# A fixed instruction order with 59 exceptions, and a 512-wide last projection, in a fused attention and SwiGLU block

## The chip, the cores and the metric

The kernel runs on one core of a Trainium2 chip. The metric is the device time of one execution in microseconds (us). Ratios are given with a 95% interval. Engines are named as in the profile: PE (matmul), PEld (weight load), DVE (vector), ACT (activation), POOL and SP (which issues nearly all DMAs).

## The reference, cut to what matters

```python
S, D, H, Dh, F = 2048, 1024, 32, 32, 3584
sa, ca, ga, sb, cb, gb = six rows of silu(c) @ w_mod
h = layernorm(x) * (1 + ca) + sa
q = h @ wq              # 32 heads of 32
k, v = h @ wk, h @ wv   # one head, shared by all queries
p = softmax(q k^T / sqrt(32));  o = p v
x = x + ga * (o @ wo)
h = layernorm(x) * (1 + cb) + sb
x = x + gb * ((silu(h @ w1) * (h @ w3)) @ w2)
```

Everything is bf16. Two stages matter in what follows: the softmax, whose 2048 x 2048 x 32 exponentials all go through ACT, and the feed-forward part (FFN below), which is about half of PE's work.

## The kernel before: the parts that the argument touches

The kernel is a generator. It adds each instruction to a graph with its duration, its priority and what it reads and writes; then a list scheduler walks the graph with a model of time and **fixes the order of all engines before anything runs**. On the chip each engine works through its list, waiting on semaphores.

```python
def schedule(self, banks):
    ...
    while left:
        ...                      # the engine that can start something first
        if e == "pe":
            def key(c):
                s, n = c
                if n.cls == "S":             # score groups first
                    r = 0
                elif n.cls is not None:      # V: value matmuls, D: denominators
                    r = 1 if att or t - n.est > 1.0 else 4
                else:                        # F: projections, FFN
                    r = 3 if n.prio >= 4 else 0.5
                return (r, n.prio, n.seq)
        ...
        pick = min((c for c in cands if c[0] <= t + ...), key=key)
        ...
        if e == "pe" and self.warm is not None and t < self.warm[0]:
            ...                  # fills a hole with matmuls nobody reads
```

The 2048 queries are cut into 8 blocks of 256. A block has 64 *score groups*: eight matmuls into the banks set aside for scores (SP) in PSUM, the memory that matmuls write, read by two exps on ACT. While attention of one block runs, PE also has the output projection and the FFN of the block before it. All of this other work shares two PSUM banks (PB). Copying a result out of a bank is called its eviction.

```python
PB = [nc.alloc_psum_tensor("PB%d" % i, [P, 512], F32)[:] for i in range(2)]
...
def finish(f, h=None):            # for 4 heads (f) of a block
    g = grp()                     # takes one of the banks
    ...
        G.add("pe", vmm, ..., cls="V", mode="V", acq=g if w0 == 0 else None, groups=[(g, "w")])   # L983
    ...
        G.add("pe", dmm, ..., groups=[(g, "w")], mode="V", cls="D")                               # L1010
    ...
    G.add("dve", ... tensor_copy(ASB[:, f % 4, 0:qn], PB[g.bank][:, 0:qn]),
          groups=[(g, "r")], prio=1)                                                              # L1022
    ...
    G.add("dve", ... tensor_tensor(DSB[:, da, 0:qn], DSB[:, da, 0:qn], PB[g.bank][:, qn:2 * qn], ALU.add),
          groups=[(g, "r")], prio=1)                                                              # L1034
```

So the numerators and the denominators of four heads lie in one bank, and the bank is free only when DVE has copied the one (L1022) and added the other (L1034). Whoever comes next on PE and wants a bank waits for that.

The FFN of a block: the first two projections by tiles of 256 columns of `w1` and `w3`, each into a slot of a ring of six weight slots, then the second projection in four quarters of 256 columns, then two stores of 128 rows:

```python
for fp in range(NF // 2):
    sl, rk = ring()
    for w, src in enumerate((w1_in, w3_in)):
        dma(..., src[:, c0:c0 + 256] ..., ("ring", sl, w), nbytes=D * 512, clear=rk)
    for w in range(2):
        g = mm_group(2 * NC, gmm, ...)               # L1149, 16 matmuls of 256 columns
        ...                                          # DVE and ACT: tanh form of silu, product
for q in range(4):
    g = grp()
    for hf in range(2):
        dma(...)                                     # half of a quarter of w2
        ...                                          # L1183: 28 matmuls of 256 columns
    ...                                              # L1189, L1195: times gb, plus x
for t in range(t0, t0 + nt):
    dma(lambda e, t=t: e.dma_start(out2[t * P:(t + 1) * P, :], X[:, xs(t), :]), ...)   # L1201
```

The changed kernel has other line numbers. The same work stands at:

| work | before | after |
|---|---|---|
| score groups / exps | L923 / L933 | L960 / L970 |
| value matmuls / denominators | L983 / L1010 | L1026 / L1053 |
| DVE: numerators out / denominators added | L1022 / L1034 | L1065 / L1077 |
| query projection on PE / eviction by DVE | L663 / L666 | L700 / L703 |
| transposes on PE / eviction by DVE | L587 / L610 | L624 / L647 |
| first FFN projections | L1149 | L1199 |
| second projection, narrow / wide | L1183 / none | L1270 / L1241 |

The softmax here doesn't subtract the row's maximum and nothing guards it: scores larger than these inputs give would overflow.

## Time and profile before

| | before |
|---|---|
| median (lowest to highest) | 1147.71 us (1146.38 to 1148.85), 3 runs |
| span in the profile | 1144.24 us |
| start of score groups 1, 91, 129, 449 | 26.58, 199.81, 276.59, 907.15 us |
| start of the first FFN matmul, end of the last matmul | 199.49, 1139.82 us |
| from one block to the next (64 score groups) | 126.11 us |

The starts of score groups are a good ruler for this kernel: there are 512 of them, every kernel below has the same ones in the same order, and a difference between two kernels can be placed between two of them. "S91" below is the start of the 91st.

### The profile page before, as it was taken

How to read it: one execution, taken by the hardware profiler on the slowest of the kernel's cores; microseconds unless marked ns; L12 is line 12 of the kernel's file. 1: busy time of each engine (PE TensorE's matmuls, PEld its weight loads, DVE VectorE, ACT ScalarE, POOL GpSimd, SP SyncE). 2: the span in 40 equal slices, each digit the busy share in tenths (PEclk: the TensorE clock that was granted, in tenths of full speed). 3: DMA queues.
4: the chain of work that ended last, by engine and by line, in shares of the span. 5: the costliest groups of instructions: out<-in, count | busy, mean ns of one | idle time of the engine just before them, and what ended most of it. 6: DMA issues, size and time to landing. Idle time of an engine off the chain costs nothing.

```text
span 1144.2 us, 35491 instructions
## 1 busy us (share of the span) xinstructions
PE 1114.2 (97%) x15800; PEld 758.0 (66%) x15830; DVE 985.3 (86%) x1501; ACT 1024.9 (90%) x1167; POOL 43.6 (4%) x86
## 2 busy tenths in 40 slices
PE   7898998999999999999999999999999999999998
PEld 4564443767577666777567757776677757767887
DVE  6838899899989998999989998999989999997451
ACT  5999999999999999999999999999999999992110
POOL 3200001000100001000100000000100010000000
PEclk9999999999999999999999999999999999999999
DMA  9616102965596567865596558756785659656995
GB/s 331 191 58 203 39 1 66 286 190 168 121 294 190 163 172 193 232 172 164 151 254 199 163 144 237 206 165 183 163 250 169 183 121 282 196 154 187 293 292 152
DMA packets 385417, 211.09 MB, mean 184 GB/s; under 512 B 21745, under 2 KB 376049, under 8 KB 385265
## 3 DMA queue, kind: packets, MB, share of 16 engines
q1 hardware_dynamic: 383184, 208.69, 66.1%
q8 instruction: 124, 2.03, 0.8%
q10 hardware_dynamic: 2080, 0.13, 0.1%
q14 instruction: 29, 0.23, 0.1%
HBM read 201.46 MB, written 4.19 MB: 180 GB/s over the span
## 4 chain that ended last, share of the span: by engine, by line
PE 84%; ACT 9%; DVE 4%; POOL 1%; issue 1%; DMA 0%; SPq 0%
PE PB L1149 30%; PE PB L1183 16%; PE SP L923 12%; PE PB L983 10%; ACT UREG L933 8%; PE PB L1115 4%; PE SP L1149 3%; PE PB L663 3%; PE SP L1183 2%; PE PB L1010 2%; DVE UREG L956 1%; DVE QT L666 1%; DVE UREG L950 1%; DVE ST L530 0%; POOL RS L553 0%
## 5 line engine op out<-in xcount | busy, mean ns | idle before, releaser
L933 ACT ACTIVATE UREG<-SP 128x1024 bf16<-128x1024 f32 x1024 | 969.2, 1085 | 7.1 <-PE SP L923 5.2
L956 DVE TENSOR_TENSOR UREG<-UREG 128x2048 bf16<-128x2048 bf16 x240 | 292.4, 1218 | 11.1 <-ACT UREG L933 8.7
L1149 PE MATMUL PB<-QT,WREG 128*128 128x256 bf16 x1648 | 206.8, 273 | 2.0 <-DVE DSB L1034 2.0
L923 PE MATMUL SP<-QT,KT 32*128 32x256 bf16 x4096 | 203.5, 273 | 4.9 <-ACT UREG L933 4.7
L1149 PEld LDWEIGHTS PB<-QT,WREG 128*128 128x128 bf16 x1648 | 150.1, 98 | 46.6 <-issue 30.9
L950 DVE TENSOR_TENSOR UREG<-UREG 128x2048 bf16<-128x2048 bf16 x120 | 146.3, 1219 | 9.6 <-PE PB L1010 5.1
L923 PEld LDWEIGHTS SP<-QT,KT 32*128 32x128 bf16 x4096 | 60.8, 92 | 128.4 <-ACT UREG L933 75.4
L1149 PE MATMUL PB<-QT,HREG 128*128 128x256 bf16 x1056 | 134.1, 273 | 0.9 <-DVE DSB L1034 0.8
L983 PE MATMUL PB<-UREG,V 128*32 128x256 bf16 x4032 | 129.4, 274 | 3.4 <-DVE QT L610 1.2
L1149 PEld LDWEIGHTS PB<-QT,HREG 128*128 128x128 bf16 x1056 | 96.0, 98 | 30.1 <-issue 20.1
L983 PEld LDWEIGHTS PB<-UREG,V 128*32 128x32 bf16 x4032 | 98.1, 96 | 26.6 <-issue 17.7
L1183 PE MATMUL PB<-WREG,HREG 128*128 128x256 bf16 x812 | 100.6, 273 | 0.0
L1183 PEld LDWEIGHTS PB<-WREG,HREG 128*128 128x128 bf16 x812 | 75.5, 98 | 19.9 <-issue 11.0
L1149 PE MATMUL PB<-QT,X 128*128 128x256 bf16 x528 | 67.9, 274 | 0.0
L1183 PE MATMUL PB<-HREG 128*128 128x256 bf16 x532 | 67.3, 273 | 0.0
L663 PE MATMUL PB<-HREG,WREG 128*128 128x512 bf16 (+1 forms) x299 | 61.5, 338 | 3.7 <-DVE QT L666 1.6
L1158 ACT ACTIVATE GSB<-GSB 128x512 bf16<-128x512 bf16 x56 | 39.7, 709 | 27.5 <-DVE GSB L1156 27.5
L965 DVE TENSOR_TENSOR UREG<-UREG 128x2048 bf16<-128x2048 bf16 x52 | 63.4, 1219 | 0.6
L551 POOL TENSOR_SCALAR RS<-MV 128x1 f32<-128x1 f32 x32 | 20.6, 649 | 1004.2 <-DVE MV L532 1004.0
L1183 PEld LDWEIGHTS PB<-HREG 128*128 128x128 bf16 x532 | 49.3, 98 | 13.7 <-issue 7.8
L1158 ACT ACTIVATE WREG<-WREG 128x512 bf16<-128x512 bf16 x56 | 39.9, 713 | 20.0 <-DVE WREG L1156 20.0
L1149 PEld LDWEIGHTS PB<-QT,X 128*128 128x128 bf16 x528 | 48.2, 98 | 14.5 <-issue 9.5
(141 smaller groups left out, 1043.0 us busy)
## 6 DMA issues: line engine op xcount, KB each, us to landing
WREG<-in_B_w_dram SPq DMA_DIRECT2D x112, 512.0 KB, 5.3
HREG<-in_B_w_dram SPq DMA_DIRECT2D x74, 512.0 KB, 5.3
WREG<-in_B_w_dram SPq DMA_DIRECT2D x33, 896.0 KB, 5.1
X<-in_B_w_dram SPq DMA_DIRECT2D x38, 512.0 KB, 5.6
HREG<-in_B_w_dram SPq DMA_DIRECT2D x21, 896.0 KB, 5.1
X<-in_B_w_dram SPq DMA_DIRECT2D x10, 896.0 KB, 5.2
X<-in_A_x_dram SPq DMA_DIRECT2D x32, 256.0 KB, 5.3
WREG<-in_w_mod_dram SPq DMA_DIRECT2D x16, 512.0 KB, 4.6
```

Source lines behind the costliest of these rows:

```text
L663: g = mm_group(NC, lambda e, b, c: e.matmul(b[:, 0:n], WQ[:, c, f * P:(f + 1) * P], HT[:, c, sl], start=c == 0, stop=c == NC - 1), lambda ...
L923: r = e.matmul(SP[:, b, o:o + qn], KT[32 * gg:32 * gg + 32, kts[j] * P:(kts[j] + 1) * P], QT[32 * gg:32 * gg + 32, f, q0:q0 + qn], start=T ...
L933: G.add("act", lambda e, u=u, h0=h0, n=n, b0=b0, nb=nb: e.activation(U[:, u, h0 * W:(h0 + n) * W].rearrange("p (b w) -> p b w", b=nb), SP[ ...
L950: G.add("dve", lambda e, tr=tr, u=u, fu=first_u: e.tensor_tensor(TR[:, tr, 0:4 * W], U[:, fu, 0:4 * W], U[:, u, 0:4 * W], ALU.add), reads= ...
L956: G.add("dve", lambda e, tr=tr, u=u: e.tensor_tensor(TR[:, tr, 0:4 * W], TR[:, tr, 0:4 * W], U[:, u, 0:4 * W], ALU.add), reads=[("TR", tr) ...
L965: G.add("dve", lambda e, ta=ta, tb=tb: e.tensor_tensor(TR[:, ta, 0:4 * W], TR[:, ta, 0:4 * W], TR[:, tb, 0:4 * W], ALU.add), reads=[("TR", ...
L983: r = e.matmul(PB[g.bank][32 * gg:32 * gg + 32, 0:qn], V[:, kt, :], U[:, pu, (gg * npk + j) * qn:(gg * npk + j + 1) * qn], start=w0 + n == ...
L1010: r = e.matmul(PB[g.bank][32 * gg:32 * gg + 32, qn:2 * qn], SEL[:, ga, gj, :], a[:, (gg * npk + x % npk) * qn:(gg * npk + x % npk + 1) * q ...
L1115: g = mm_group(NC, lambda e, b, f, t=t, h=h: e.matmul(b, QT[:, f, t * P:(t + 1) * P], WO[:, f, h * 512:(h + 1) * 512], start=f == 0, stop= ...
L1149: return e.matmul(b[:, j * qn:(j + 1) * qn], w13[:, w, c, j * P:(j + 1) * P], QT[:, c, q0:q0 + qn], start=c == 0, stop=c == NC - 1)
L1158: G.add("act", lambda e, b=b: e.activation(TB[b], GS[b], ACT.Tanh, scale=0.5), reads=[("GS", b)], writes=[("TB", b)], clear=alias("TB") if ...
L1183: G.add("pe", lambda e, g=g, j=j, fc=fc, hf=hf, first=first, w2s=w2s: e.matmul(PB[g.bank][:, j * 256:(j + 1) * 256], HHT[:, hf * NH + fc, ...
```

## The change

Intent: let the order depart from the scheduler's rule in 59 places that a search had found, and make the last block's end shorter.

The scheduler numbers its choices. Where another kind of instruction could start at the same time, the entry of `CH` under that number says which alternative is taken; without an entry the rule holds. On DVE one alternative (`None`) is to hold the engine for 0.3 us.

```diff
+CH = {88: 2, 187: 1, 188: 1, 196: 1, 205: 1, 224: 1, 229: 1, 262: 1, 329: 2, 352: 1, 362: 1, 375: 1, 411: 1,
+      442: 1, 609: 2, 654: 2, 662: 1, 731: 1, 775: 1, 851: 2, 1272: 1, 1290: 2, 1463: 1, 1478: 1, 1492: 1, 1497: 1,
+      1526: 1, 1897: 1, 1915: 2, 2088: 1, ... , 3772: 1, 3790: 2,
+      3963: 1, 3978: 1, 3992: 1, 3997: 1, 4009: 1, 4163: 1, 4339: 1, 4342: 1, 4490: 1}
...
+    def choose(self, t, e, n, alts):
+        self.nch += 1
+        return CH.get(self.nch - 1, 0)
...
+            ch = self.choose(t, e, n, alts) if alts else 0
+            if ch:
+                if alts[ch - 1] is None:
+                    t_free[e] = t + 0.3
+                    continue
+                s, n = alts[ch - 1]
```

The second part loads weights for two tiles at a time (`w1` of both, then `w3` of both), and gives the buffers of the two tiles other places:

```diff
-        for fp in range(NF // 2):
-            sl, rk = ring()
+        for fd in range(NF // 4):
+            ws = []
+            for b in range(2):
+                sl, rk = ring()
+                ...
             for w, src in enumerate((w1_in, w3_in)):
-                dma(...)
+                for sl, rk, w13, c0 in ws:
+                    dma(...)
```

The third part is for the last block alone (`WIDE = (2,)`). Its second projection is 512 columns wide, in halves of four weight chunks, and each [128 x 512] of the output is stored as soon as it is done:

```diff
+        if wide:
+            NH = NF // 4
+            for h in range(2):
+                ...                                  # four chunks of w2, 512 columns each
+                for j in range(nt):
+                    g = grp()
+                    ...                              # 28 matmuls of 512 columns, L1241
+                    G.add("dve", ... O2B[:, ob], PB[g.bank], GBB[:, h * 512:(h + 1) * 512], ALU.mult ...)
+                    G.add("dve", ... X[:, sj, h * 512:(h + 1) * 512] ... ALU.add ...)
+                    dma(lambda e, ...: e.dma_start(out2[t * P:(t + 1) * P, h * 512:(h + 1) * 512], ...), ...)
```

Other additions of the diff (a second fold, a tanh over two tiles) are switched off.

## The prediction

> **What bounds the kernel now.** I read the page's totals and chain first, then the busy time by stretch, then the timeline at three places.
>
> ```profile
> PE 1114.2 (97%) x15800; PEld 758.0 (66%) x15830; DVE 985.3 (86%) x1501; ACT 1024.9 (90%) x1167; POOL 43.6 (4%) x86
> ...
> PE 84%; ACT 9%; DVE 4%; POOL 1%; issue 1%; DMA 0%; SPq 0%
> ```
>
> ACT at 90% is not a rival to PE over the whole span: it finishes its exps long before the end. The stretches (columns: PE, PEld, DVE, ACT, POOL busy with counts, clock, DMA share, GB/s) show where PE has holes:
>
> ```profile
> 122.00:163.00 41.00, 38.88 (x507) 17.69 (x512) 36.13 (x56) 40.39 (x44) 0.00 (x0) 1.00 0.01 2
> 180.00:200.00 20.00, 16.68 (x280) 8.19 (x280) 19.10 (x26) 19.35 (x22) 0.65 (x2) 1.00 0.34 90
> 200.00:1032.00 832.00, 827.70 (x11832) 567.22 (x11837) 772.59 (x1117) 828.92 (x942) 20.59 (x24) 1.00 0.70 192
> 1066.00:1140.00 74.00, 73.82 (x677) 65.90 (x674) 33.60 (x51) 8.81 (x14) 0.00 (x0) 1.00 0.98 249
> ```
>
> Before 200 us PE waits; after that it is full. The timeline of a middle block shows that the fullness is real:
>
> ```profile
> 600.37 2.03 PE L1149 MATMUL PB<-QT,HREG 128*128 128x256 bf16 x17
> 602.34 0.40 PE L923 MATMUL SP<-QT,KT 32*128 32x256 bf16 x8
> 602.66 1.27 PE L1149 MATMUL PB<-QT,HREG 128*128 128x256 bf16 x10
> ```
>
> From the starts: 17 matmuls and the change to the score group take 1.97 us, the score group and the change back 0.32. I went through the starts of all matmuls of this block: apart from one wait of about 0.2 us before an output projection and a gap of missing records, every step is 0.11 us, or 0.20 us where the tiling changes. **From the first FFN matmul (199.49 us) to the last (1139.8 us) the time is the sum of PE's work in its order.** ACT runs at 99.6% beside it, but no PE instruction waits for it beyond the cost of the change.
>
> Before 199.5 us the two alternate. Here (block 0's end):
>
> ```profile
> 151.66 0.40 PE L923 MATMUL SP<-QT,KT 32*128 32x256 bf16 x8
> 151.99 1.93 PE L983 MATMUL PB<-UREG,V 128*32 128x256 bf16 x64
> 153.85 0.40 PE L923 MATMUL SP<-QT,KT 32*128 32x256 bf16 x8
> 154.30 15.15 ACT L933 ACTIVATE UREG<-SP 128x1024 bf16<-128x1024 f32 x16 [0.25 <-PE SP L923]
> ...
> 196.05 0.40 PE L923 MATMUL SP<-QT,KT 32*128 32x256 bf16 x8 [0.47 <-ACT UREG L933]
> ```
>
> A lump of 64 value matmuls holds the next score group to 2.19 us, and ACT starves for 0.25; elsewhere PE waits 0.47 for ACT. One score group feeds two exps; the chain of waits has "230.20 7.33 ACT UREG L933 x8", so 0.917 us an exp and 1.834 us a group.
>
> **What the Trainium skill says.** "Perfetto Trace Analysis", Identifying the Most-Contended Engine: matmul busy share is not a good measure of nearness to the limit; therefore I used starts, not the 97%. "TensorE: Matmul & The Clock Gate", Back-to-back issue gap: N/2.4 + 2.5 ns when warm, so 109.2 ns for 256 columns and 215.8 for 512. The trace agrees: 56 matmuls in 6.11 us in the chain, and 24 of 512 columns in 5.18 us. "TensorEngine Tiling (Array Packing)", Key Properties: changing the tiling mode drains the engine. The trace agrees: about 0.09 us a change. "DMA: Bandwidth & Descriptors", Anatomy of one DMA: about 2.0 us fixed. The next-to-last output store took 2.04 us from issue to landing.
>
> **The change part by part.** I compared the built instruction orders, counting PE's groups. No arithmetic is taken out, except that the last block's second projection is 112 matmuls of 512 columns instead of 224 of 256.
>
> 1. *Picks before the first FFN matmul.* Both kernels do all query projections before it. I took each interval between score groups as the larger of 1.834 us and its PE content (0.216 us a 512-column matmul, 0.109 a 256, 0.027 a tile-packed one, 0.093 a change of tiling). Sums over intervals 1-20, 21-30, 31-50, 51-71, 72-80, 81-90: before 38.0, 19.7, 37.5, 40.5, 17.4, 18.5 = 171.6; after 37.9, 18.8, 37.4, 39.9, 16.9, 18.5 = 169.4. The trace has 173.2 (26.58 to 199.81 us), so the count misses 1.6 us of waits for other engines. The gain, 2.2 us, comes from lumps such as the 64 value matmuls, now cut in two around a score group (1.80 and 1.81 us of content, both hidden by the exps), and from query projections kept for the wait behind block 0's output projection, where the kernel before runs fillers (45 filler matmuls in all before, 38 after). But the first FFN matmul now follows the 91st score group instead of coming just ahead of it: 199.81 - 2.2 + 0.33 + 0.22 (one filler) = 198.2, so **-1.3 us** against 199.49.
> 2. *Waits that the count misses.* About 0.8 of the 1.6 us lies at intervals 81 and 82 (2.28 and 2.19 us for contents of 1.75 and 1.15), where value matmuls stand behind a transpose and wait for DVE's eviction. After, the transposes are split and the value work stands elsewhere. I take about half of the 1.6: **-0.7**.
> 3. *Picks from there on.* One score group fewer is left (-0.22); changes of tiling 924 before, 925 after (+0.09). The middle blocks have 141 changes each instead of 139, which the last block gives back. So the five picks that recur in every middle block are worth nothing on PE: **-0.1**. That 202 instead of 226 matmuls of block 6 remain after the last score group only moves ACT's end; PE does the same work.
> 4. *Wide second projection.* 224 x 0.1092 = 24.46 against 112 x 0.2158 = 24.17: **-0.3**. It reads four weight chunks in 6 us in its first pass, so they must be there early; six ring slots give it that.
> 5. *Stores per half.* The end now:
>
> ```profile
> 1139.86 0.69 DVE L1189 TENSOR_TENSOR WREG<-PB,GBB 128x512 bf16<-128x512 f32 x1 [4.96 <-PE PB L1183]
> 1140.58 0.42 DVE L1195 TENSOR_TENSOR X<-X,WREG 128x512 bf16<-128x512 bf16 x1
> 1141.04 0.83 SPq L1201 DMA_DIRECT2D out_dram<-X  x2
> ```
>
> The second store is issued 0.39 us behind the first and lands 2.7 us after 1141.04. After, one store of half the size remains: no second issue, and some 0.3 us less to move. **-0.8**.
>
> Sum: -3.2 us of 1147.7, so 1144.5.
>
> **Rivals.** *A new wait in the middle.* DVE is 93% busy there and the order on every engine is fixed; a moved addition that ends late would stop PE seven times. For: five picks recur per block, and cutting value lumps brings bank releases nearer to their users. Against: the kernel before shows hardly a wait in such a block. At 0.3 us a block: +2, so 1146.5. *The search hits more than I count*: PE's waits and fillers before 200 us are some 15 us by my sum; if a third goes, 1142. *The weight stream becomes the bound at the end*: it runs at about 290 GB/s from 1060 to 1120 us, DMA share above 1; loads are now issued in pairs of tiles, and the wide pass wants 3.7 MB at twice the pace. Against: no PE wait for a DMA there now, and 1 KB rows instead of 512 bytes. If it misses, +2 to +5 us. *ACT bounds the middle*, so a smoother exp stream counts: 126.1 us a block against 128 x 0.917 + 14 x 0.52 = 124.6 would give 1.5 us a block, 10 in all. Against: PE shows no wait to give back.
>
> **Range and chances.** The parts are each uncertain by about 1 us, the runs before spread over 2.5 us, and the rivals pull both ways: 1144.5 with 1141.5 to 1147.4. Two per cent is 23 us; the waits and the tail together hold less than that, so faster by 2% is nearly excluded, and slower by 2% needs a stall of 3 us in each block, which nothing suggests.
>
> **What would show it.** Step 1: the 91st score group near 197 us, first FFN matmul near 198. Step 3: a middle block still 126.1 to 126.3 us, PE without waits. Step 4: the last projection in 24.2 us without a gap. Step 5: from last matmul to the end 3.6 us instead of 4.4. The prediction is wrong if a block's period falls below 125.5 us (then ACT, not PE, bounded it) or rises above 126.8 (a new wait).

## More of the kernel before

The prediction reads the totals, the stretches and the timeline. Here is a view that it doesn't show: what PE waited for. The columns are what waited and its line, what it waited for, the sum in us, how many times, and the longest.

```profile
PE SP L923 <- ACT UREG L933: 4.7, 12, 0.7
PE PB L1149 <- DVE DSB L1034: 2.8, 7, 0.4
PE PB L663 <- DVE QT L666: 1.6, 3, 0.8
PE PB L983 <- DVE QT L610: 1.2, 1, 1.2
PE PB L1115 <- issue: 1.1, 7, 0.2
PE PB L983 <- DVE QT L666: 1.1, 1, 1.1
```

Read it by the count in the middle. Twelve waits of 4.7 us in total are PE waiting for exps. The third, fourth and sixth line are PE waiting for DVE to empty a bank, a few times in the whole execution. The second line and the fifth come seven times, and so does the FFN beside an attention block: eight blocks, and all but the last have their FFN beside the next one's attention.

## The result, and the profile after

The changed kernel takes **1139.26 us** (median of 6 runs, 1138.17 to 1139.95), the kernel before 1147.21 in the same rounds (6 runs, 1146.38 to 1148.85). The ratio is 0.9929, 95% 0.9916 to 0.9942. The gain of 7.9 us is real, under two per cent, and more than twice the 3.2 us predicted; 1139.26 lies below the range.

Totals and chain of the changed kernel's page, beside those in the prediction:

```profile
PE 1117.9 (98%) x15711; PEld 745.9 (66%) x15711; DVE 986.4 (87%) x1501; ACT 1021.6 (90%) x1167; POOL 41.4 (4%) x86
...
PE 84%; ACT 12%; DMA 2%; DVE 1%; POOL 1%; issue 0%; SPq 0%; DVEq 0%
```

DVE's share of the chain fell from 4% to 1%, and DMA's rose from 0% to 2%. Both point to something below. The stretches (PE, PEld, DVE, ACT, POOL busy with counts, clock, DMA share, GB/s):

```profile
180.00:200.00 20.00, 16.91 (x281) 8.76 (x281) 19.97 (x27) 20.00 (x23) 0.00 (x0) 1.00 0.44 114
200.00:1032.00 832.00, 831.80 (x11850) 569.71 (x11851) 775.88 (x1121) 824.92 (x938) 19.58 (x24) 1.00 0.70 193
```

In the second row PE is busy for 831.80 of 832.00 us. The row of the kernel before, in the prediction, has 827.70. I had read that as full; it had a hole of 4.3 us by the profile's own count.

**What the hole was.** The timeline of a middle block of the kernel before (start, duration, engine, line, operation, output and input, count, and in brackets the idle time before and who ended it):

```profile
642.58 0.39 PE L1010 MATMUL PB<-UREG,SEL 128*32 128x256 bf16 x8
...
642.91 0.40 PE L923 MATMUL SP<-QT,KT 32*128 32x256 bf16 x8
643.03 0.42 DVE L1022 COPY XN<-PB 128x256 f32<-128x256 f32 x1 [0.50 <-PE PB L1010]
...
643.24 0.28 PE L1149 MATMUL PB<-QT,X 128*128 128x256 bf16 x1
643.37 0.41 DVE L1034 TENSOR_TENSOR DSB<-DSB,PB 128x256 f32<-128x256 f32 x1
...
643.92 0.82 PE L1149 MATMUL PB<-QT,WREG 128*128 128x256 bf16 x6 [0.41 <-DVE DSB L1034]
```

From the last matmul of one FFN group (643.24) to the first of the next (643.92) it is 0.69 us in the unrounded starts, where 0.11 is the usual step: 0.58 us lost. (The bracket says 0.41, since it counts from the modelled end of the matmul.) The new group needs a bank; one is held by the group that has just ended, the other by the values and denominators, and it is free when the addition at L1034 ends, at 643.78. When I wrote the prediction I took this step for missing records. The waits view names it, seven times: 2.8 us by its way of counting, and 7 x 0.58 = 4.1 us by starts. So the hole of 4.3 us isn't made of this alone: 2.8 us of it are these waits, and most of the rest are gaps of 0.16 us before output projections, where a record is missing and no time was lost (below). That 4.1 and 4.3 lie close together is chance.

The same place in the changed kernel:

```profile
640.12 0.40 PE L960 MATMUL SP<-QT,KT 32*128 32x256 bf16 x8
...
640.45 0.62 PE L1026 MATMUL PB<-UREG,V 128*32 128x256 bf16 x16
...
640.89 0.39 PE L1053 MATMUL PB<-UREG,SEL 128*32 128x256 bf16 x8
...
641.22 0.83 PE L1199 MATMUL PB<-QT,WREG 128*128 128x256 bf16 x6
...
641.98 0.40 PE L960 MATMUL SP<-QT,KT 32*128 32x256 bf16 x8
```

Behind the denominators there are now six matmuls of an FFN group that already has its bank, then a score group; the bank is asked for later, when DVE is done. No bracket is left. The block's period fell from 126.11 to 125.77 us: 0.58 given back, less two more changes of tiling in a block (141 instead of 139, some 0.09 us each), which leaves 0.40 where 0.34 was measured.

What PE waits for in the changed kernel, the lines that answer to those above:

```profile
PE SP L960 <- ACT UREG L970: 5.7, 15, 1.1
...
PE PB L1199 <- DMA WREG<-in_B_w_dram: 1.2, 1, 1.2
...
PE PB L700 <- DVE QT L703: 0.5, 1, 0.5
```

The addition of denominators is gone from the list, waits for the query projection's eviction are down from 1.6 and 1.1 us to 0.5, and there is a new line: one wait for a weight load. It stands at the first FFN tile:

```profile
198.44 0.40 PE L960 MATMUL SP<-QT,KT 32*128 32x256 bf16 x8 [0.46 <-ACT UREG L970]
200.08 2.91 PE L1199 MATMUL PB<-QT,WREG 128*128 128x256 bf16 x13 [1.24 <-DMA WREG<-in_B_w_dram]
202.92 0.61 PE L960 MATMUL SP<-QT,KT 32*128 32x256 bf16 x8
```

PE now reaches `w3` of the first tile before the load has landed. A second thing is to be seen here: 13 matmuls took 2.91 us, where 13 x 0.109 and the change of tiling are about 1.5. PE ran at half its clock for 3.41 us from 200.2 us on. That is not part of the change; other profiles here have it at other places or not at all, and it cost this one about 1.8 us (below).

The end of the changed kernel:

```profile
1134.73 0.69 DVE L1247 TENSOR_TENSOR WREG<-SP,GBB 128x512 bf16<-128x512 f32 x1 [4.61 <-PE SP L1241]
1135.52 0.42 DVE L1251 TENSOR_TENSOR X<-X,WREG 128x512 bf16<-128x512 bf16 x1
1135.97 0.33 SPq L1254 DMA_DIRECT2D out_dram<-X  x1
```

The DVE work is as long as before, but one store of half the size is left and landed 1.70 us after issue. From the last matmul (1134.69) to the end of the span (1138.16) it is 3.47 us, before it was 4.42.

### The profile page after: what moved, and what is told of

Read it like the earlier page. It is cut to its first block, busy times and chain, and to the rows that moved or that the text cites. A ratio compares the mean times of both kernels' runs of the same rounds, so it can differ in the third digit from the quotient of the medians.

```text
span 1138.2 us, 35291 instructions
## 1 busy us (share of the span) xinstructions
PE 1117.9 (98%) x15711; PEld 745.9 (66%) x15711; DVE 986.4 (87%) x1501; ACT 1021.6 (90%) x1167; POOL 41.4 (4%) x86
## 4 chain that ended last, share of the span: by engine, by line
PE 84%; ACT 12%; DMA 2%; DVE 1%; POOL 1%; issue 0%; SPq 0%; DVEq 0%
PE PB L1199 29%; PE PB L1270 14%; PE SP L960 13%; ACT UREG L970 12%; PE PB L1026 9%; PE PB L1158 5%; PE PB L700 3%; PE SP L1199 3%; PE SP L1270 2%; PE PB L1053 2%; PE SP L1241 1%; PE PB L1241 1%; DMA WREG<-in_B_w_dram 1%; ACT WREG L1207 1%; PE SP L1158 1%; DMA WREG<-in_w_mod_dram 1%
## 5 line engine op out<-in xcount | busy, mean ns | idle before, releaser
L1026 PE MATMUL PB<-UREG,V 128*32 128x256 bf16 x4096 | 132.9, 274 | 1.2 <-ACT UREG L970 1.0
L1207 ACT ACTIVATE WREG<-GSB 128x512 bf16<-128x512 bf16 x112 | 74.9, 669 | 45.1 <-DVE GSB L1204 45.1
L1270 PE MATMUL PB<-WREG,HREG 128*128 128x256 bf16 x700 | 88.6, 273 | 0.0
L1270 PEld LDWEIGHTS PB<-WREG,HREG 128*128 128x128 bf16 x700 | 64.0, 98 | 19.2 <-issue 11.8
L1219 DVE SCALAR_TENSOR_TENSOR HREG<-WREG,HREG 128x512 bf16<-128x512 bf16 x112 | 75.8, 677 | 0.9
L1204 DVE CAST GSB<-PB 128x512 bf16<-128x512 f32 x104 | 70.7, 680 | 4.4 <-PE PB L1199 3.5
L1214 DVE TENSOR_TENSOR HREG<-GSB,PB 128x512 bf16<-128x512 bf16 x98 | 66.3, 676 | 6.0 <-PE PB L1199 5.6
L700 PE MATMUL PB<-HREG,WREG 128*128 128x512 bf16 (+1 forms) x312 | 65.1, 340 | 0.9 <-DVE QT L703 0.5
L1270 PE MATMUL PB<-HREG 128*128 128x256 bf16 x476 | 61.2, 273 | 0.0
```

Source lines behind the costliest of these rows:

```text
L700: g = mm_group(NC, lambda e, b, c: e.matmul(b[:, 0:n], WQ[:, c, f * P:(f + 1) * P], HT[:, c, sl], start=c == 0, stop=c == NC - 1), lambda ...
L1026: r = e.matmul(PB[g.bank][32 * gg:32 * gg + 32, 0:qn], V[:, kt, :], U[:, pu, (gg * npk + j) * qn:(gg * npk + j + 1) * qn], start=w0 + n == ...
L1204: G.add("dve", lambda e, g=g, b=b: e.tensor_copy(GS[b][:, 0:2 * qn], PB[g.bank][:, 0:2 * qn]), writes=[("GS", b)], groups=[(g, "r")], dur= ...
L1207: G.add("act", lambda e, b=b: e.activation(TB[b], GS[b], ACT.Tanh, scale=0.5), reads=[("GS", b)], writes=[("TB", b)], clear=alias("TB"), d ...
L1219: G.add("dve", lambda e, fp=fp, b=b: e.scalar_tensor_tensor(HHT[:, 2 * fp:2 * fp + 2, 0:qn], TB[b][:, 0:2 * qn].rearrange("p (j q) -> p j ...
L1270: G.add("pe", lambda e, g=g, j=j, fc=fc, hf=hf, first=first, w2s=w2s: e.matmul(PB[g.bank][:, j * 256:(j + 1) * 256], HHT[:, hf * NH + fc, ...
```

## The experiments

Theories, by the letters that the expectations use. **A**: the picks ahead of the first FFN matmul are most of the gain; the picks that recur in every block give 0.35 us each, and the last projection and its stores 1.2. **B**, the rival: the picks of the middle blocks are most of it, 4 us or more. **C**: the layout does it (weight loading in pairs, buffers, the wide projection), not the order. The prediction itself had held a fourth view, that the middle picks are worth nothing. The later calls have theories of their own, on the load and on the start. Four kernels on one chip, five rounds each, with the kernel before at 1147.72 us (9 runs).

### No picks at all

```diff
-CH = {88: 2, 187: 1, ... , 4490: 1}
+CH = {}
```

> The changed kernel with the 59 picks taken out: wide last projection, half stores, paired weight loads and the new sigmoid buffers alone. Theory A (the picks in the first 200 us remove PE's waits and ACT's hunger, and that is most of the gain): 1146.0 us, that is 1.2 under the kernel before (0.3 for the wide matmuls, 0.9 for the last store), the 91st score group at 199.8 us and a middle block at 126.1. Theory B (the picks of the middle blocks do it): the same 1146.0. Theory C (the layout does it, not the order): 1141 or less.

Measured: 1146.26 us (1145.62 to 1146.73), ratio 0.9984 (0.9972 to 0.9997). The blocks' period is 126.11 us as before, the wait for the denominators is there seven times, and the last stretch, from S449 to the last matmul, takes 232.39 us instead of 232.67. So the wide projection gives 0.28 us, the half stores shorten the tail from 4.42 to 3.48, and C falls: without picks 1.2 us by the trace (1.5 by the medians) is all there is. A and B both had 1146.0, so this run doesn't separate them. The profile had a stretch at half clock at 105.5 us.

### Only the picks up to number 851

```diff
-CH = {88: 2, ... , 851: 2, 1272: 1, ... , 4490: 1}
+CH = {88: 2, ... , 851: 2}
```

> Only the 21 picks that fall before the first FFN matmul. Theory A: the 91st score group at 194.8 us as in the changed kernel, the first FFN matmul at 195.3, about 4 us below the kernel without picks, so 1142.0; less what the late weight load at 198 us takes back. Middle blocks at 126.1. Theory B: at most 1 to 2 us below the kernel without picks, so 1144.5.

Measured: 1142.11 us (1140.97 to 1145.54), ratio 0.995 (0.9936 to 0.9963). Of the waits of PE:

```profile
PE PB L1199 <- DVE DSB L1077: 2.4, 6, 0.4
...
PE PB L1199 <- DMA WREG<-in_B_w_dram: 0.9, 1, 0.9
```

The list has 20 entries, not the 21 of the expectation. The wait for the load is there, and without picks it wasn't, so the early picks bring it about. The wait for the denominators is there six times of seven, and the period is 126.11. By the medians the gain is 5.6 us, where the changed kernel has 7.9; what is missing must come from later picks. The profiled execution, 1145.54, is the slowest of the five: it had three units of 3.41 us at half clock, from 37.9 and 102.7 us.

### All but the last nine picks

```diff
-CH = {88: 2, ... , 3790: 2, 3963: 1, 3978: 1, 3992: 1, 3997: 1, 4009: 1, 4163: 1, 4339: 1, 4342: 1, 4490: 1}
+CH = {88: 2, ... , 3790: 2}
```

> All picks but the last nine, those of the last block. Theory A: the middle blocks go to 125.77 us, 0.35 less each in five blocks, so about 1.5 below the kernel with the early picks: 1140.5. The rest to 1139.3 is the last block. Theory B: the step from the early picks to this one is 4 us or more.

Measured: 1140.69 us (1139.11 to 1141.02), ratio 0.9932 (0.9919 to 0.9944). The period is 125.76, and of the two waits in question this is left:

```profile
PE PB L1199 <- DMA WREG<-in_B_w_dram: 1.0, 1, 1.0
...
PE PB L1199 <- DVE DSB L1077: 0.4, 1, 0.4
```

The one that is left stands at 1016 us, in the last block, whose picks were taken away. B is refuted, since the step from the early picks is 1.4 us by the medians and not 4, and so is the prediction's own view: blocks whose picks are kept lose the wait and 0.35 us of their period, and the block whose picks are gone keeps the wait. From S449 to the last matmul it is 232.04 us, against 231.13 in the changed kernel: the last nine picks are worth 0.91 us, of which 0.58 is the wait, and three changes of tiling fewer (928 to 925 from the first FFN matmul on) are about 0.3.

### The last projection narrow again

```diff
-    WIDE = (2,)
+    WIDE = ()
```

> The changed kernel with all picks, but the last block's second projection 256 wide and its rows stored whole. The orders of all engines are the same up to that projection. Theories A and B: 0.3 for the matmuls and 0.9 for the store are lost, 1140.5 us. Theory C: 3 us or more are lost.

Measured: 1139.79 us (1139.42 to 1141.27), ratio 0.9933 (0.992 to 0.9945). In the trace the last stretch is 0.29 us longer (231.42 instead of 231.13) and the tail is 4.42 us again instead of 3.48; from S449 to the end of the span it is 235.84 us, in the changed kernel 234.62. The medians show 0.5 against the changed kernel. It was run at another time. Medians don't resolve this here, the trace does. C, which had 3 us or more, falls here too.

On another chip: what the wait for the load costs, and whether it can be had back. The kernel before took 1146.54 us there (9 runs). All of these five-round runs keep the changed kernel's order on PE, ACT and DVE.

### The changed kernel again

> The changed kernel once more, unchanged, beside the next three on the same chip: 1139.3 us. If its profile holds no stretch at half clock, the 129th score group is at 272.5 us instead of 274.3, and the span about 1136.5.

Measured: 1139.03 us (1138.48 to 1140.07), ratio 0.9931 (0.9917 to 0.9944), as in the first measurement. PE waits 0.9 us for the load, and this time runs at full clock there. Its stretch at half clock is elsewhere:

```profile
98.00:101.80 3.80, 3.15 (x69) 1.77 (x68) 3.46 (x5) 3.10 (x5) 0.00 (x0) 1.00 0.56 182
101.80:105.20 3.40, 3.40 (x18) 0.90 (x16) 2.56 (x5) 2.75 (x4) 0.00 (x0) 0.51 0.96 329
```

The column behind POOL is the granted clock: 1.00, then 0.51 for 3.4 us, with PE busy through all of it. Interval S31 to S51 is 38.85 us here and 37.00 to 37.12 in profiles of the same order without such a stretch, so it costs 1.7 to 1.9 us. With one in the profile, the expected span of 1136.5 wasn't put to the test.

### `w3` of the first tile ahead of `w1` of the second

```diff
+    u, v = firstw[1], firstw[2]    # the 2nd and 3rd weight load of the first FFN
+    sp[u.pos], sp[v.pos] = v, u    # exchanged in the DMA queue, after scheduling
```

> The changed kernel with two weight loads of the first FFN exchanged in the DMA queue (the first tile's second weight ahead of the second tile's first), every engine's order frozen. Theory A (what the early picks won is partly given back by a late weight load at 198 us): PE's wait of 1.2 to 1.3 us for that load goes, the way from the 91st to the 129th score group falls from 77.8 to about 76.9, and the time is 1 us lower, 1138.3. Rival (that wait lies beside ACT's pace and costs nothing): no change.

Measured: 1138.41 us (1137.85 to 1139.38), ratio 0.9927 (0.9915 to 0.994). The same place as above:

```profile
199.72 0.40 PE L960 MATMUL SP<-QT,KT 32*128 32x256 bf16 x8 [0.46 <-ACT UREG L970]
200.05 1.59 PE L1199 MATMUL PB<-QT,WREG 128*128 128x256 bf16 x13
```

No bracket stands on the second line any more, and 13 matmuls take 1.59 us. S91 to S129 is 76.95 us, against 77.6 to 77.8 in the profiles with the wait and without half clock there, and 76.78 in the kernel before. So the wait costs 0.7 to 0.9 us, most of the 0.8 to 1.1 that the waits view shows for it in those profiles, and the rival falls. It takes two things together: PE that comes earlier (without picks there is no such wait) and the pairing, by which `w3` of the first tile stands third in the queue.

### The first tile's weights in a slot that is free early

```diff
+    RING[0], RING[5] = RING[5], RING[0]    # the first tile takes the slot that is free from about 50 us
...
+    for n, (was, now) in firstw[:12]:      # after scheduling: wait for the old contents of the new slot
+        n.deps = [d for d in n.deps if id(d) not in was] + list(now.values())
+    # and the first loads sorted anew in the DMA queue, both of the first tile in the two early places
```

> The changed kernel with the first tile's weights in the ring slot that is free from about 50 us (the sixth tile's stood there), every engine's order frozen. Theory A: the first FFN matmuls never wait for a load, 1 to 1.3 us lower than the changed kernel, 1138.0; with fewer stretches at half clock perhaps 1137.5. Rival: the sixth tile's load now comes in the crowded queue and makes PE wait near 215 us instead: no gain or a loss.

Measured: **1137.85 us** (1137.73 to 1139.91), ratio 0.9925 (0.9913 to 0.9938). No wait for a load is left, S91 to S129 is 76.96 us. Four of the five runs lie at 1137.7 to 1137.9; the fifth has a mean clock of 0.998 and 1139.91. This is the best version of the study, and beats both kernels: its median is 1.2 us below the changed kernel's of the same call. The intervals of the two ratios overlap, so it is the trace, with 0.7 to 0.9 us less between S91 and S129, that says where it comes from. Part of the rest is half clock: among the runs with a mean clock of 1.000 the two kernels are 1.06 us apart (1137.82, four runs, and 1138.88, three). The load of the sixth tile made PE wait nowhere, so the rival falls.

### Only the picks up to 442

```diff
-CH = {88: 2, ... , 442: 1, 609: 2, ... , 4490: 1}
+CH = {88: 2, ... , 442: 1}
```

> Only the 14 picks up to number 442, which reach to about the 50th score group. Theory A: the way to the 51st group is as in the changed kernel, 1.8 us shorter than before; of the rest of the 5.0 us at the 91st group (1.5 between groups 51 and 72, 0.4 to 81, 1.3 to 91) most is missing, so the 91st group is near 198 us where no half clock falls. Rival (the first picks set up all that follows): the 91st group at 195.

One look: 1142.65 us. S91 stands at 196.65, with a stretch at half clock before it, so about 195 without: the rival was right. I had expected that a part of S91's gain would need the picks from 609 on; it doesn't, and the builds show that picks numbered over 442 change nothing on PE ahead of the 92nd group. So the question of what sets up the gain at the start is one about the first 14 picks.

Three shorter lists, with one run of the kernel before at 1145.96 us. They were run at other times.

### Only the first pick; the first 8; the first 12

```diff
-CH = {88: 2, ... , 4490: 1}
+CH = {88: 2}                               # p88
+CH = {88: 2, 187: 1, ... , 262: 1}         # p262
+CH = {88: 2, 187: 1, ... , 375: 1}         # p375
```

> The first pick alone (it moves vector statistics and some value projections among score groups 3 to 15). Counting PE's content by interval, as in the prediction, it is worth 0.1 us; if it also takes away waits, as I now think, the 21st score group comes 0.6 us earlier, at 38.05 us after the first, and the 91st at 172.6 after the first (173.2 before). A stretch at half clock adds 1.4 to 2 us where it falls, and is told from the clock records.

> The first eight picks. By the count of contents 1.4 us of the 2.2 at the 91st score group. If the picks' real worth is the waits, the way from the first to the 31st group is 56.7 us (58.4 before), but from the 81st to the 91st it is still about 19 us, since value matmuls stand behind the transposes there: the 91st at 170.5 to 171.5 after the first.

> The first twelve picks. The twelfth puts query projections and split transposes between groups 81 and 88, so the way from the 81st to the 91st falls from 19.3 to 18.0 us; the 91st group 168.4 us after the first, as good as all picks (168.2). Rival (the last two early picks hold a share): 169.5.

Measured: 1146.56, 1145.47 and 1141.26 us, single runs. The intervals between score groups tell more (us; a star marks a stretch at half clock inside, which adds 1.4 to 1.9):

| groups | before | first 1 | first 8 | first 12 | first 14 | all |
|---|---|---|---|---|---|---|
| 1 to 21 | 38.63 | 40.55* | 40.06* | 38.71 | 40.00* | 38.05 |
| 21 to 31 | 19.79 | 19.79 | 18.62 | 18.55 | 18.54 | 18.63 |
| 31 to 51 | 37.18 | 37.30 | 37.43 | 37.02 | 37.02 | 37.12 |
| 51 to 72 | 41.00 | 41.00 | 40.36 | 39.50 | 39.47 | 39.48 |
| 72 to 81 | 17.34 | 17.34 | 18.43 | 16.92 | 16.90 | 16.90 |
| 81 to 91 | 19.29 | 19.28 | 18.66 | 18.13 | 18.03 | 18.03 |
| sum | 173.23 | 175.26* | 173.56* | 168.83 | 169.96* | 168.21 |

The first pick alone moves nothing that can be seen (the interval that it could change is hidden by the half clock). The first eight shorten 21 to 31 by 1.2 and 51 to 72 by 0.6, and lose 1.1 at 72 to 81; a new wait of 2.0 us of a score group for an eviction (L647) stands at 189 us, within 81 to 91. Without the half clock S91 would come some 171.6 to 172.2 us after S1, later than the 170.5 to 171.5 expected. With four more, 173.23 becomes 168.83: nearly all of the early gain, as expected. The last two add at most 0.6, and the first interval alone scatters by 0.4 between profiles with all picks (38.05 to 38.47). So the early gain isn't one event: the first eight picks give about a quarter of it, and with those from 329 to 375 nearly all is there. Whether the latter would give their part without the first eight wasn't tested.

## Why the prediction was wrong

The sum of terms, without half clock, in us. "Measured" is from the traces of before and after and of the experiments.

| term, by the prediction's steps | predicted | measured |
|---|---|---|
| steps 1 and 2, at the first FFN matmul | -2.0 | -4.2 |
| the same, at S91 | | -5.0 |
| late first weight load, S91 to S129 | 0 | +0.9 to +1.0 |
| step 3, S193 to S449 (four blocks) and the last stretch without its own nine picks | -0.1 | -1.4 and -0.35 |
| step 3, the last block's picks | in the above | -0.9 |
| step 4, wide projection | -0.3 | -0.3 |
| step 5, tail | -0.8 | -0.9 |
| sum (from S91: -5.0 + 0.95 - 1.4 - 0.35 - 0.9 - 0.3 - 0.9) | -3.2 | -7.9 |

The -5.0 is the difference of two profiles; four others with all early picks and no half clock there (to 3790, narrow, and the two with moved loads) have S91 at 168.3 to 168.6 us after S1, so 4.6 to 4.9.

**What bounds the kernel: right but for 4.1 us, by one wrong sentence.** PE's work in its order does set the time from the first FFN matmul on, all but seven waits; ACT at 99.6% did not keep the period from falling. The sentence that failed is "apart from one wait of about 0.2 us before an output projection and a gap of missing records, every step is 0.11 us, or 0.20 us where the tiling changes". I had the two exchanged. The "gap of missing records" was the wait of 0.58 us for the denominators, seven times over. The "wait of about 0.2 us" before the output projection was the missing record: one matmul of 512 columns takes 0.216 us, and the count there is one short. The waits view had both, on its second and fifth line; the second is said to be ended by DVE, the fifth by "issue", that is by nothing.

**Steps 1 and 2 together had 2.9 us at S91, and it was 5.0.** By stretches as in step 1, the count of content had 0.1, 0.9, 0.1, 0.6, 0.5 and 0 us; the traces fell by 0.6, 1.2, 0.1, 1.5, 0.4 and 1.3. Step 1's method has a flaw: taking the larger of ACT's 1.834 us and PE's content in each interval *by itself* overcounts, since where PE has little to do it runs ahead of ACT (in the kernel before, S88 comes 1.63 us after S87), and what it has put in front of ACT covers a longer interval after it. So 171.6 is too large, and the 1.6 us of waits that step 2 took from it is too small. How the 5.0 us divide into content and waits over the whole way stays open.

**Step 2 failed: "I take about half of the 1.6: -0.7".** What the traces show beyond the content that step 1 counted is 5.0 - 2.2 = 2.8 us. The clearest part is S81 to S91: the prediction counted the same content before and after, 18.5 us; PE's waits for DVE there fell from 2.1 to 0.2 us, and the time from 19.29 to 18.03, so 1.3 us went in this stretch alone. On the whole way from S1 to the first FFN matmul the waits view sums up PE's waits for DVE to 5.6 us before and 1.6 us after; not all of a wait is lost time where ACT has work in stock. Here are two of them in the kernel before, where the prediction saw only the intervals that held them:

```profile
182.80 0.40 PE L923 MATMUL SP<-QT,KT 32*128 32x256 bf16 x8
184.44 0.62 PE L983 MATMUL PB<-UREG,V 128*32 128x256 bf16 x16 [1.24 <-DVE QT L610]
...
187.29 0.62 PE L587 MATMUL PB<-IDENT,XN 128*128 128x128 bf16 x8
188.38 0.59 PE L663 MATMUL PB<-HREG,WREG 128*128 128x512 bf16 x2 [0.47 <-DVE DSB L1031]
```

PE stands for 1.24 us because both banks are waiting for DVE. The next score group starts at 184.99, 2.19 us after this one instead of 1.834, so about 0.36 us of the 1.24 is lost, and ACT stands idle for 0.26. The mechanism of step 2 was right and its example was this very place; the size was wrong by a factor of about four (0.7 for 2.8, if step 1's 2.2 is let stand), since I took it as the remainder of a sum that was too large.

**Step 3 failed: "the five picks that recur in every middle block are worth nothing on PE: -0.1".** They are worth 0.35 us a block, and the last block's 0.9. (By the list there are seven entries a block.) I had counted PE's matmuls and changes of tiling, which do not change for the better, and asked no further because of the sentence above: where no wait is seen, none can be taken away. The test that I wrote down did its work, though: the period was to stay at 126.1 to 126.3, and 125.77 shows the step wrong. It did not fall below 125.5, so by the prediction's own test ACT did not bound it; its rival "ACT bounds the middle" had 1.5 us a block, and 0.34 was measured.

**Steps 4 and 5: right**, each to 0.15 us: the 112 wide matmuls start 215.8 ns apart, and the last store lands 1.70 us after its issue, where in the kernel before the second of two landed 2.31 us after its own, issued 0.39 us behind the first.

**The rivals.** "The search hits more than I count" had the right direction and, for the start, about the right size (a third of some 15 us); it named 1142, and had nothing on the blocks after the start. "A new wait in the middle" was wrong in sign: a wait was there and was taken away. "The weight stream becomes the bound at the end" did not happen; the weight stream struck at the start instead, once, for 0.7 to 0.9 us, because PE came to the first tile earlier while `w3` had moved back in the queue. Nothing in the prediction had asked whether work brought forward would find its weights.

**What stays open.** Stretches of 3.41 us at half clock, starting near 38, 102 to 105 or 200 us, are in seven of the twelve profiles of the changed kernel and its variants. Each costs 1.4 to 1.9 us, and runs with a mean clock of 0.998 instead of 1.000 are 1 to 2 us longer, so they account for a good part of the spread within each kernel. Runs of the kernel before have such clocks too, though its one profile has no such stretch before its last matmul. What sets them off wasn't tested.

## What to carry to other kernels

When an engine looks full, go through every step that is longer than usual with the waits view beside it, and call it missing records only where a count of instructions proves it: a wait of 0.58 us in each block hid as one. Where two engines alternate and one can queue ahead, don't take the larger of the two by the interval; let the queue carry over, and see in the waits view what each wait costs the other engine. And when a change brings work forward, ask what it will wait for next: here the first weight load, and one exchange in the DMA queue gave most of the loss back.

## What the Trainium skill lacked or had wrong

- "TensorE: Matmul & The Clock Gate", What's actually happening, has the half rate as the default that follows an idle window of about 3.4 us. Here stretches of 3.41 us at half clock came in the middle of the work without such an idle window: in the changed kernel PE had waited 0.46 and 1.24 us in the 3.4 us before 200.2 us, and in its repeat it was busy for 3.15 of the 3.8 us before 101.8 us. A later section, A second HAM failure mode, does have frequent short idle times between groups of matmuls bring it about, but the page gives no measure of how much activity is enough.
- The same page, Back-to-back issue gap, gives a sustained rate of about 131 ns a matmul for 512 columns beside its formula. Here only the formula held: 215.8 ns for 512 columns with new weights for each.
- "TensorEngine Tiling (Array Packing)", Key Properties, says that a change of mode drains the engine, and no cost. Here it is about 0.09 us each, so the 1127 changes of the kernel before are about 100 us of PE's time, an estimate from these two numbers.
- "DMA: Bandwidth & Descriptors" has a fixed cost only for DMAs issued by GpSimd (in Anatomy of one DMA), and none for those that SP issues. Here stores issued by SP took 1.70 us from issue to landing for 128 KB, and 2.04 and 2.31 us for 256 KB, all at the end of the kernels.
- "Perfetto Trace Analysis" has no test to tell a missing record from a wait. Here a wait of 0.58 us was taken for the one, and a missing record of 0.216 us for the other.
